# VectorE makes all low halves of the experts' weights and all one-hot tiles of the late plan

## The chip, the cores and the metric

The program runs on one core of a Trainium2 chip. The core has a matrix engine (TensorE, PE in the profile; its weight loads are PEld), VectorE (DVE), ScalarE (ACT), GpSimd (POOL), a queue engine that issues transfers (SyncE, SP) and 16 DMA engines. Each engine works through its own queue of instructions in order, and semaphores order the engines among each other. The metric is the device time of one execution in microseconds (us); lower is better.

## The reference

Three layers follow each other on 2304 tokens of width 512; everything is float32.

```python
scores = scale * q @ k.T, masked (local in 4 heads, strided in 4), softmax, @ v     # attention, 4 x 8 heads
h = x @ w_in; g = max(h, 0) + alpha * min(h, 0); x = g @ w_out                      # 512 -> 2048 -> 512
e_idx = argmax(x @ w_gate); gate_w = softmax value of that expert                   # 8 experts
out[tokens of e] = gate_w * sigmoid(x @ w_output_gate)[e] * (max(x @ w1[e], 0) @ w2[e])   # 512 -> 1024 -> 512
```

## The kernel before

A float32 product is made on TensorE as three products of split operands: each operand is written as a high half (rounded to the fast float format) and a low half (the difference), and high*high, low*high and high*low are summed. So each weight tile has to be split before it is used: ScalarE writes the high half by a copy, and another engine subtracts it from the raw tile.

The tokens go through the attention and the first MLP in six blocks of 384. As soon as five blocks are done, the routing is planned for them ("early" plan), and the last block follows while the first experts are at work ("late" plan). A plan ranks the tokens of each expert, gives each token a place in a list, and makes the lists by matmuls (function `lists`): for each of 18 (early: 15) tiles of 128 tokens a one-hot matrix of 128x128 (`onehot`, from the low part of the rank, `rank_lo`) is multiplied with a small matrix `aa`. The late plan is cut into five steps; the table `WHEN` says at which place of the loop over the experts each of them is written.

The experts are worked off in 16 places `t` in a fixed order: four early pairs of 128 tokens (kind P), then S0 Q0 S1 S2 P0 S3 Q1 P1 Q3 P2 Q2 S4. A P place has two lists of 128 tokens, an S place one, a Q place one of 32. For place `t` the loop writes the first product of place `t+1`, the second product of `t`, and the weight splits of `t+1` and `t+2`.

The weights of one expert are 4 MB: four raw tiles of 1 MB (`raws[0..3]`, one buffer each), loaded by SP in program order (`load_expert`, L884, skipped where the expert is the same as that of the place before). `split_expert(t, h)` splits one half of them into four tiles `wx`: ScalarE's copy (L891), then the subtraction (L893), which for `i == 3` is on GpSimd and else on VectorE. A raw tile can be loaded again when both subtractions of its two halves have read it, so raw tiles 1 and 3 wait for GpSimd. GpSimd's queue has the gathers of tokens (L900), the scatters of results (L1057) and 12 of the late plan's one-hot tiles (L794, `OHP`) as well; VectorE makes the other 6.

The names used below: `exh`, `exl` are the transposed tokens of a place (L911 transposes into the bank `sl_bank`, L924 writes the high half, L926 the low half), L955 to L959 and L970 to L972 are the first product (the middle one or the last one of three reads `exl` or the weights' low half), L994, L995, L1016 and L1017 split the hidden layer (`hh`, `hl`), L1015 transposes it into the banks X and T, L1047 is the second product, L806 the list matmuls.

Of the kernel before, what the change touches and what calls it, by code (L numbers as in the profile page):

```python
# [7 lines left out]
F32 = mybir.dt.float32  # L8
# [4 lines left out]
ALU = mybir.AluOpType  # L13
# [13 lines left out]
NTT = NT // P  # L27
BLK = 384
NBLK = NT // BLK
TPB = BLK // P  # L30
# [23 lines left out]
XA = 3  # L54

WHEN = ((0, 7), (1, 1), (1, 1), (1, 4), (1, 6))
OHP = 12

NRV = range(FIRST)
FS = {2: 2}  # L60
# [24 lines left out]
def attention_prelu_mlp_routed_experts_kernel(  # L85
# [11 lines left out]
    nc = tc.nc  # L97
# [28 lines left out]
    with tc.manual_schedule():  # L126
# [4 lines left out]
        def bank(tag, bufs=1):  # L131
            return ps.tile([P, 512], F32, tag=tag, name=tag, bufs=bufs)
# [3 lines left out]
        def half(tag):  # L136
            return sl_bank[:, 0:256] if tag == "S" else sl_bank[:, 256:512]
# [475 lines left out]
        def rank(blk):  # L613
            j0 = blk * TPB
            sl = slice(j0, j0 + TPB)

            def small(shape, name, dt=F32):
                return xpool.tile(shape, dt, tag=name, name=name, bufs=1)

            tmp = small([P, TPB, E], "r_tmp")  # L620
            pr_ = half("L") if blk < NBLK - 1 else bank("acc0")
            pr3 = pr_[:, : TPB * E]
            mm(pr3, u16, oh[:, sl, :].rearrange("p j e -> p (j e)"), start=True, stop=False)
            mm(pr3, one16, acc_oh[:, sl, :].rearrange("p j e -> p (j e)"), start=False, stop=True)
            rk = small([P, TPB], "r_rk")
            nc.vector.tensor_tensor(
                out=tmp, in0=pr3.rearrange("p (j e) -> p j e", e=E), in1=oh[:, sl, :], op=ALU.mult
            )
            nc.vector.tensor_reduce(out=rk, in_=tmp, axis=X, op=ALU.add)
            rh = rank_hi[:, sl]  # L630
            nc.vector.tensor_scalar(
                out=rh, in0=rk, scalar1=1.0 / P, scalar2=-63.5 / P, op0=ALU.mult, op1=ALU.add
            )
            nc.vector.tensor_scalar(out=rh, in0=rh, scalar1=BIG, scalar2=BIG, op0=ALU.add, op1=ALU.subtract)
            nc.vector.scalar_tensor_tensor(
                out=rank_lo[:, sl], in0=rh, scalar=-float(P), in1=rk, op0=ALU.mult, op1=ALU.add
            )

        plan_t = {}

        def plan_parts(early):
# [6 lines left out]
            nt = NTT - TPB if early else NTT  # L648
# [4 lines left out]
            def small(shape, dt=F32):  # L653
                n = 1
                for d in shape[1:]:
                    n *= d
                w = n if dt == F32 else (n + 1) // 2
                t = room[: shape[0], room_at[0] : room_at[0] + w]
                room_at[0] += w
                if dt != F32:  # L660
                    t = t.bitcast(dt)[:, :n]
                if len(shape) == 3:
                    t = t.rearrange("p (a b) -> p a b", b=shape[2])
                return t
# [46 lines left out]
            else:  # L711
# [8 lines left out]
                    out=two, in0=two, scalar1=2 * BIG, scalar2=2 * BIG, op0=ALU.add, op1=ALU.subtract  # L720
# [29 lines left out]
            if early:  # L750
                aa = small([P, nt, 2 * ns], BF16)
            else:
                room2 = stage()
                aa = room2[:, : nt * ns].bitcast(BF16).rearrange("p (a b) -> p a b", b=2 * ns)
# [4 lines left out]
                out=aa[:, :, ns:], in0=a, scalar1=cst[:, C_P1 : C_P1 + 1], scalar2=None, op0=ALU.mult  # L759
# [6 lines left out]
            def experts(c0, c1, cum):  # L766
                n = c1 - c0
                t = le[:, c0 - k0 : c1 - k0]
                tt(
                    t,  # L770
                    cum[0:1].unsqueeze(1).to_broadcast([1, n, E]),
                    isl[0:1, c0:c1].unsqueeze(2).to_broadcast([1, n, E]),
                    ALU.is_le,
                )
                r = ef[:, c0 - k0 : c1 - k0]
                nc.vector.tensor_reduce(out=r, in_=t, axis=X, op=ALU.add)
                nc.vector.tensor_scalar_min(e_i32[:, c0:c1], r, float(E - 1))
# [3 lines left out]
            else:  # L781
                experts(C_P, C_S, cum)
                experts(C_S, C_Q, cum1)
                experts(C_Q, NSLOT, cumq)
            yield
            tag, w = ("xg", DM + 1) if early else ("gh", BLK)
            k = 2 * w // P
            onehot = []
            for j in range(nt):
                if j % k == 0:  # L790
                    pool = epool if early else xpool
                    t = pool.tile([P, w], F32, tag=tag, name="onehot", bufs=XG if early else 3).bitcast(BF16)
                onehot.append(t[:, (j % k) * P : (j % k + 1) * P])
                (nc.vector if early or j >= OHP else nc.gpsimd).tensor_scalar(  # L794
                    out=onehot[j], in0=i128, scalar1=rank_lo[:, j : j + 1], scalar2=None, op0=ALU.is_equal
                )
            plan_t[early] = aa, small, onehot

        def lists(early):
            k0, k1 = (0, EARLY) if early else (EARLY, NSLOT)  # L800
# [85 lines left out]
        def split_expert(t, h, some=range(4)):  # L886
            for i in some:
                q = 4 * h + i
                raw = raws[q // 2][:, (q % 2) * 1024 : (q % 2) * 1024 + 1024]
                w = wx[t, q] = w_tile(NA, F32R, "wx")  # L890
                nc.scalar.activation(out=w[:, :1024], in_=raw, func=AF.Copy)  # L891
                eng = nc.gpsimd if i == 3 else nc.vector
                eng.tensor_tensor(out=w[:, 1024:], in0=raw, in1=w[:, :1024].bitcast(F32), op=ALU.subtract)  # L893

        xg_t, wt_t, xx_t, hp_t, hr_t, hh_t, po_t = {}, {}, {}, {}, {}, {}, {}

# [237 lines left out]
        for s in range(NPRO):  # L1134
# [5 lines left out]
            if s == 4:  # L1140
# [3 lines left out]
                    out=wg_hl[:, :, 2 * E :], in0=wg_sb, in1=wg_hl[:, :, : 2 * E].bitcast(F32), op=ALU.subtract  # L1144
# [149 lines left out]
        for t in range(NPL):  # L1294
            more = t + 1 < NPL
            wide_now = kinds[t] == "P"
            wide_next = more and kinds[t + 1] == "P"
            few_now = kinds[t] == "Q"
            few_next = more and kinds[t + 1] == "Q"
            if t < 2:  # L1300
                gathers(XA, EARLY // 2)
            else:
                gathers(XA)
            if wide_next:
                first_product(t + 1, range(2))
            if few_next:
                first_product(t + 1)
                if t + 2 < NPL:
                    load_expert(t + 2, 0)
            late_turn = few_now and more and not wide_next  # L1310
            if late_turn:
                first_product(t + 1)
                relu(t + 1, 0)
            nb = NB.get(kinds[t] + kinds[t + 1] + kinds[t + 2], 2) if t + 2 < NPL else 2
            split(t + 2, 0, range(nb))
            at(t, 1)
            early_x = wide_next and t + 2 < NPL and kinds[t + 2] == "Q"
            if early_x:
                turn_x(t + 2, 0)
            if more and not few_next and not late_turn:  # L1320
                first_product(t + 1, range(2, 4))
            at(t, 2)
            if late_turn:
                relu(t + 1, 1)
            if t + 2 < NPL and not early_x:
                turn_x(t + 2, 0)
            if late_turn:
                turn_h(t + 1)
            elif more and not wide_next:
                relu(t + 1)  # L1330
            elif more and not wide_now:
                relu(t + 1, 2)
                relu(t + 1, 3)
            split(t + 2, 0, range(nb, 4))
            at(t, 3)
            if not few_now:
                second_product(t, 0, 4)
            if few_next:
                turn_h(t + 1)
            at(t, 4)  # L1340
            if wide_now and wide_next:
                relu(t + 1, 2)
                relu(t + 1, 3)
            if t == 0:
                rank(NBLK - 1)
            if t + 2 < NPL and kinds[t + 2] == "P":
                turn_x(t + 2, 1)
            at(t, 5)
            if not few_now:
                second_product(t, 4, 8)  # L1350
            at(t, 6)
            if t == 3:
                others = value(idx_any)
            if not few_now:
                split(t + 1, 1)
                give(t)
            at(t, 7)
            if few_next:
                second_product(t + 1, 0, 8)
                if t + 2 < NPL:  # L1360
                    load_expert(t + 2, 1)
                if t > 2:
                    gathers(XA)
                split(t + 2, 1)
                give(t + 1)
            elif more and not wide_next and not late_turn:
                turn_h(t + 1)
# [132 lines left out]
```

## Time and profile before

| what | us |
|---|---|
| median of 3 runs | 815.4 (814.32 to 817.51) |
| the profiled execution | 815.9 |
| its span, first to last instruction | 814.0 |
| PE busy | 782.4 (96%) |
| DVE busy | 456.3 (56%) |
| ACT busy | 428.1 (53%) |
| POOL busy | 167.0 (21%) |

The rows below come from one profiled execution. Times of rows are counted from the start of the span. PE is busy nearly all the time, so the stretches where it is not are what there is to look for; a row of waits tells which engine ended them, and a timeline row what that engine did before.

### The profile page before, as it was taken

The numbers are of one execution on the slowest core, as the hardware profiler recorded it, in microseconds if no ns is written. First come the engines' busy times: TensorE is split into PE (matmuls) and PEld (weight loads), VectorE is DVE, ScalarE is ACT, GpSimd is POOL, SyncE is SP. The second block draws the span as 40 slices with busy tenths as digits, with TensorE's granted clock in tenths as the row PEclk, the third lists the DMA queues.
The fourth block names the chain that finished last, engine by engine and source line by source line (L and its number), as shares of the span: only waits on it lengthen the run. The fifth ranks groups of instructions, "written<-read, shape, count | busy, mean of one in ns | idle before, by whom it ended". The sixth has DMA issues, their size and how long they took to land. (4 is left out here: it accounts for less than half of the span.)

```text
span 814.0 us, 13678 instructions
## 1 busy us (share of the span) xinstructions
PE 782.4 (96%) x5046; PEld 657.5 (81%) x5050; DVE 456.3 (56%) x1005; ACT 428.1 (53%) x1057; POOL 167.0 (21%) x127
## 2 busy tenths in 40 slices
PE   8888999999999999999999999999989998999995
PEld 4566778888888888888888888899879876878884
DVE  5989994345434544545334335566695447854422
ACT  6867875554445454645333343364444566665542
POOL 0001111010101010111000000133365454536422
PEclk9899999999999999999999999999999999999998
DMA  9719212012100120101000001635033677777520
GB/s 342 312 50 365 79 39 79 1 38 81 65 0 19 68 84 32 47 1 40 1 0 19 22 1 40 246 117 177 19 106 141 212 253 273 268 276 267 182 83 32
DMA packets 22621, 91.05 MB, mean 112 GB/s; under 512 B 3082, under 2 KB 7312, under 8 KB 15376
## 3 DMA queue, kind: packets, MB, share of 16 engines
q1 hardware_dynamic: 18816, 78.52, 27.4%
q0 software_dynamic: 3728, 11.55, 4.0%
q8 instruction: 42, 0.69, 0.4%
q14 instruction: 35, 0.29, 0.1%
HBM read 105.78 MB, written 9.97 MB: 142 GB/s over the span
## 5 line engine op out<-in xcount | busy, mean ns | idle before, releaser
L444 PE MATMUL h<-xh,w 128*128 128x384 f32 x384 | 129.8, 338 | 1.1 <-DVE gl L465 0.8
L445 PE MATMUL h<-xl,w 128*128 128x384 f32 x384 | 129.2, 337 | 0.7 <-DVE xl L373 0.7
L446 PE MATMUL h<-xh,w 128*128 128x384 f32 x384 | 129.2, 336 | 0.0
L893 DVE TENSOR_TENSOR wx<-raw,wx 128x1024 fp32r<-128x1024 f32 x72 | 97.0, 1391 | 50.0 <-ACT wx L891 49.7
L478 PE MATMUL acc<-w,gh 128*128 128x512 f32 x288 | 124.8, 433 | 0.0
L455 DVE SCALAR_TENSOR_TENSOR h<-h,nalpha,a 128x384 f32<-128x384 f32 x96 | 59.9, 624 | 114.8 <-ACT h L454 114.7
L480 PE MATMUL acc<-w,gl 128*128 128x512 f32 x288 | 114.2, 397 | 0.0
L479 PE MATMUL acc<-w,gh 128*128 128x512 f32 x288 | 113.9, 396 | 0.0
L298 POOL TENSOR_TENSOR p<-p,sm 96x512 f32<-96x512 f32 (+2 forms) x38 | 35.6, 937 | 345.0 <-DVE sm L297 239.5
L453 ACT ACTIVATE a<-h 128x384 f32<-128x384 f32 x96 | 47.1, 491 | 103.1 <-PE h L446 103.1
L891 ACT ACTIVATE wx<-raw 128x1024 fp32r<-128x1024 f32 x96 | 94.6, 1056 | 10.7 <-DMA raw<-in_wexp_dram 10.7
L1047 PE MATMUL acc<-wx,hh 128*128 128x512 f32 x304 | 96.7, 399 | 0.0
L893 POOL TENSOR_TENSOR wx<-raw,wx 128x1024 fp32r<-128x1024 f32 x24 | 63.5, 2647 | 93.0 <-ACT wx L891 92.9
L444 PEld LDWEIGHTS h<-xh,w 128*128 128x128 f32 x384 | 72.4, 189 | 6.5 <-DVE gl L465 1.8
L445 PEld LDWEIGHTS h<-xl,w 128*128 128x128 f32 x384 | 72.3, 188 | 4.8 <-DVE xl L373 1.0
L446 PEld LDWEIGHTS h<-xh,w 128*128 128x128 f32 x384 | 72.2, 188 | 0.0
L465 DVE TENSOR_TENSOR gl<-h,gh 128x384 fp32r<-128x384 f32 x96 | 53.2, 554 | 32.0 <-PE acc L480 17.1
L1047 PEld LDWEIGHTS acc<-wx,hh 128*128 128x128 f32 x304 | 56.4, 191 | 11.1
L480 PEld LDWEIGHTS acc<-w,gl 128*128 128x128 f32 x288 | 54.5, 189 | 13.1
L464 ACT ACTIVATE gh<-h 128x384 fp32r<-128x384 f32 x96 | 46.8, 487 | 33.4 <-DVE h L455 33.1
L478 PEld LDWEIGHTS acc<-w,gh 128*128 128x128 f32 x288 | 54.2, 188 | 10.6 <-issue 0.3
L1047 PE MATMUL acc<-wx,hl 128*128 128x512 f32 x152 | 60.1, 395 | 0.0
(259 smaller groups left out, 1473.7 us busy)
## 6 DMA issues: line engine op xcount, KB each, us to landing
raw<-in_wexp_dram SPq DMA_DIRECT2D x64, 1024.0 KB
raw<-in_wp_dram SPq DMA_DIRECT2D x16, 1024.0 KB
qk<-in_qkv_dram SPq DMA_DIRECT2D x10, 576.0 KB
rows<-stage SPq DMA_DIRECT2D x15, 256.5 KB
v<-in_qkv_dram SPq DMA_DIRECT2D x8, 320.0 KB
qk<-in_qkv_dram SPq DMA_DIRECT2D x4, 384.0 KB
v<-in_qkv_dram SPq DMA_DIRECT2D x6, 256.0 KB
qk<-in_qkv_dram SPq DMA_DIRECT2D x4, 224.0 KB
```

The lines of the kernel that those rows point to most:

```text
L444: mm(ph[:, :BLK], w_in(c, 0, k), xh[:, k, :], start=(k == 0), stop=False)
L445: mm(ph[:, :BLK], w_in(c, 0, k), xl[:, k, :], start=False, stop=False)
L446: mm(ph[:, :BLK], w_in(c, 1, k), xh[:, k, :], start=False, stop=(k == KD - 1))
L453: nc.scalar.activation(out=a, in_=v, func=AF.Relu)
L455: nc.vector.scalar_tensor_tensor(out=v, in0=v, scalar=nalpha[:, c : c + 1], in1=a, op0=ALU.mult, op1=ALU.add)
L465: nc.vector.tensor_tensor(out=gl, in0=v, in1=gh.bitcast(F32), op=ALU.subtract)
L478: mm(o, gh[:, t], w_out(c, 0), start=(c == 0), stop=False)
L479: mm(o, gh[:, t], w_out(c, 1), start=False, stop=False)
L480: mm(o, gl[:, t], w_out(c, 0), start=False, stop=(c == NC1 - 1))
L891: nc.scalar.activation(out=w[:, :1024], in_=raw, func=AF.Copy)
L893: eng.tensor_tensor(out=w[:, 1024:], in0=raw, in1=w[:, :1024].bitcast(F32), op=ALU.subtract)
L1047: mm(po[i], h[:, h0 : h0 + P], wk[:, w0 : w0 + 512], start=st, stop=sp)
```

## The change

GpSimd makes no low half and no one-hot tile any more. Every `i == 3` subtraction goes to VectorE, directly behind that of `i == 2`. The one-hot tiles are made by a function of its own, `onehots`, which can be called twice: the first call, in place `t == 0` just ahead of the ranking of the last block, makes the fifteen tiles of the first five blocks (their ranks are known by then); the second, where they all stood, makes the three of the last block.

```diff
-OHP = 12
...
+            onehots(early, nt)
+            plan_t[early] = aa, small, onehot_t[early]
+
+        onehot_t = {True: [], False: []}
+        onehot_in = {}
+
+        def onehots(early, nt):
+
             tag, w = ("xg", DM + 1) if early else ("gh", BLK)
             k = 2 * w // P
-            onehot = []
-            for j in range(nt):
+            onehot = onehot_t[early]
+            for j in range(len(onehot), nt):
                 if j % k == 0:
                     pool = epool if early else xpool
                     t = pool.tile([P, w], F32, tag=tag, name="onehot", bufs=XG if early else 3).bitcast(BF16)
+                    onehot_in[early] = t
+                t = onehot_in[early]
                 onehot.append(t[:, (j % k) * P : (j % k + 1) * P])
-                (nc.vector if early or j >= OHP else nc.gpsimd).tensor_scalar(
+                nc.vector.tensor_scalar(
                     out=onehot[j], in0=i128, scalar1=rank_lo[:, j : j + 1], scalar2=None, op0=ALU.is_equal
                 )
-            plan_t[early] = aa, small, onehot
...
-                eng = nc.gpsimd if i == 3 else nc.vector
-                eng.tensor_tensor(out=w[:, 1024:], in0=raw, in1=w[:, :1024].bitcast(F32), op=ALU.subtract)
+                nc.vector.tensor_tensor(out=w[:, 1024:], in0=raw, in1=w[:, :1024].bitcast(F32), op=ALU.subtract)
...
             if t == 0:
+                onehots(False, NTT - TPB)
                 rank(NBLK - 1)
```

On VectorE, in place `t == 0` between the low halves of the hidden layer (`hl`) and the late plan's first step (`stage` is the plan's workspace), this stood in a row before:

```order
L995 SCALAR_TENSOR_TENSOR hl<-T,hh 128x512
L626 TENSOR_TENSOR r_tmp<-acc_5968,oh 128x24
L629 TENSOR_REDUCE r_rk<-r_tmp 128x3
L631 TENSOR_SCALAR rank_hi<-r_rk 128x3
L634 TENSOR_SCALAR rank_hi<-rank_hi 128x3
L635 SCALAR_TENSOR_TENSOR rank_lo<-rank_hi,r_rk 128x3
L925 COPY wt<-xg 128x1
L926 TENSOR_TENSOR exl<-sl_bank,exh 128x4x128
L893 TENSOR_TENSOR wx<-raw,wx 128x1024 x3
L668 TENSOR_SCALAR stage<-acc_6034 128x8
```

And this stands there now (line numbers are those of the changed kernel):

```order
L1002 SCALAR_TENSOR_TENSOR hl<-T,hh 128x512
L803 TENSOR_SCALAR onehot<-cst_65,rank_lo 128x128 x15
L625 TENSOR_TENSOR r_tmp<-acc_5986,oh 128x24
L628 TENSOR_REDUCE r_rk<-r_tmp 128x3
L630 TENSOR_SCALAR rank_hi<-r_rk 128x3
L633 TENSOR_SCALAR rank_hi<-rank_hi 128x3
L634 SCALAR_TENSOR_TENSOR rank_lo<-rank_hi,r_rk 128x3
L932 COPY wt<-xg 128x1
L933 TENSOR_TENSOR exl<-sl_bank,exh 128x4x128
L900 TENSOR_TENSOR wx<-raw,wx 128x1024 x4
L667 TENSOR_SCALAR stage<-acc_6052 128x8
```

Fifteen one-hot tiles now stand ahead of the ranking, of `exl` of place 2 and of the split of the weights, and that split has four subtractions where it had three.

At the end of the late plan's third step, still on VectorE, this stood before:

```order
L777 TENSOR_SCALAR e_i_4284<-stage 1x8
L794 TENSOR_SCALAR onehot<-cst_65,rank_lo 128x128 x6
L925 COPY wt<-xg 128x1
L926 TENSOR_TENSOR exl<-sl_bank,exh 128x4x128
L893 TENSOR_TENSOR wx<-raw,wx 128x1024
```

and now:

```order
L776 TENSOR_SCALAR e_i_4284<-stage 1x8
L803 TENSOR_SCALAR onehot<-cst_65,rank_lo 128x128 x3
L932 COPY wt<-xg 128x1
L933 TENSOR_TENSOR exl<-sl_bank,exh 128x4x128
L900 TENSOR_TENSOR wx<-raw,wx 128x1024 x2
```

Three one-hot tiles are left here, and the split that follows has one subtraction more.

GpSimd's queue around the same places was, from the first gathers of place 1 on:

```order
L900 DMA xg<-rows,idx_in 128x513
L893 TENSOR_TENSOR wx<-raw,wx 128x1024 x2
L605 DMA rows<-stage 128x513 x3
L900 DMA xg<-rows,idx_in 128x513 x3
L893 TENSOR_TENSOR wx<-raw,wx 128x1024 x2
L1057 DMA out_dram<-stage,idx_out 2304x512 x2
L900 DMA xg<-rows,idx_in 128x513
L794 TENSOR_SCALAR onehot<-cst_65,rank_lo 128x128 x12
L893 TENSOR_TENSOR wx<-raw,wx 128x1024 x2
L1057 DMA out_dram<-stage,idx_out 2304x512 x2
```

and is now:

```order
L907 DMA xg<-rows,idx_in 128x513 x4
L604 DMA rows<-stage 128x513 x3
L907 DMA xg<-rows,idx_in 128x513 x3
L1064 DMA out_dram<-stage,idx_out 2304x512 x2
L907 DMA xg<-rows,idx_in 128x513
L1064 DMA out_dram<-stage,idx_out 2304x512 x2
```

Only transfers are left in it; their order among themselves is the same. The queues of PE, ACT and SP hold the same instructions in the same order as before.

## Rows read from the trace of the kernel before

**Rows 1.** Busy time by stretch: length, engines' busy time (instructions), PE clock, DMA share, GB/s.

```profile
600.00:606.50 6.50, 3.19 (x26) 2.02 (x26) 6.29 (x19) 1.08 (x2) 4.91 (x6) 1.00 0.47 158
606.50:609.90 3.40, 3.40 (x11) 2.83 (x11) 3.06 (x7) 2.52 (x4) 0.00 (x0) 0.50 0.42 94
665.00:684.00 19.00, 15.44 (x72) 11.82 (x73) 12.56 (x12) 11.82 (x17) 10.91 (x6) 1.00 0.91 319
684.00:700.00 16.00, 14.33 (x102) 13.07 (x101) 14.77 (x14) 12.73 (x17) 9.82 (x5) 1.00 0.72 245
700.00:798.00 98.00, 98.00 (x795) 83.01 (x794) 46.40 (x53) 53.74 (x75) 42.23 (x26) 1.00 0.58 199
```

**Rows 2.** Waits of PE from 560 us on: sum, times, longest (us).

```profile
PE acc L957 <- DVE wx L893: 1.6, 1, 1.6
PE X L970 <- DVE hl L1017: 1.5, 1, 1.5
PE T L1015 <- ACT hr L988: 1.2, 2, 1.0
PE acc L959 <- DVE exl L926: 1.0, 1, 1.0
```

**Rows 3.** The low halves, line 893: durations in ns (min/median/max), first and last start.

```profile
L893 DVE TENSOR_TENSOR wx<-raw,wx x72: 1207/1219/3422, 530.5 to 795.4; 128x1024 fp32r<-128x1024 f32 x72
...
L893 POOL TENSOR_TENSOR wx<-raw,wx x24: 2327/2537/3200, 533.4 to 796.4; 128x1024 fp32r<-128x1024 f32 x24
```

**Rows 4.** Timeline of PE, list matmuls: start, us, instruction [idle before <-who ended it].

```profile
601.18 0.53 PE L806 MATMUL acc<-stage,onehot 128*128 128x76 bf16 x10
...
605.02 0.86 PE L806 MATMUL acc<-stage,onehot 128*128 128x76 bf16 x5 [2.12 <-DVE onehot L794]
606.33 0.80 PE L911 MATMUL sl_bank<-cst,xg 128*128 128x128 f32 x3 [0.45 <-DVE exl L926]
```

**Rows 5.** Timeline of VectorE at the early plan and at the late one.

```profile
512.35 2.51 DVE L794 TENSOR_SCALAR onehot<-cst,rank_lo 128x128 bf16<-128x128 bf16 x15
...
581.22 5.67 DVE L893 TENSOR_TENSOR wx<-raw,wx 128x1024 fp32r<-128x1024 f32 x3
...
599.53 0.50 DVE L758 TENSOR_SCALAR stage<-stage,cst 128x684 bf16<-128x684 bf16 x1
...
601.90 3.71 DVE L794 TENSOR_SCALAR onehot<-cst,rank_lo 128x128 bf16<-128x128 bf16 x6
```

**Rows 6.** Timeline of GpSimd: one-hot tiles and low halves.

```profile
592.64 9.96 POOL L794 TENSOR_SCALAR onehot<-cst,rank_lo 128x128 bf16<-128x128 bf16 x12
602.58 2.33 POOL L893 TENSOR_TENSOR wx<-raw,wx 128x1024 fp32r<-128x1024 f32 x1
...
662.17 2.39 POOL L893 TENSOR_TENSOR wx<-raw,wx 128x1024 fp32r<-128x1024 f32 x1
...
675.98 2.38 POOL L893 TENSOR_TENSOR wx<-raw,wx 128x1024 fp32r<-128x1024 f32 x1 [1.68 <-ACT wx L891]
```

**Rows 7.** Timeline of PE: where the low halves of places 2 and 8's tokens are first read.

```profile
584.12 0.28 PE L971 MATMUL h<-exl,wx 128*128 128x256 f32 x1
...
689.34 0.38 PE L971 MATMUL h<-exl,wx 128*128 128x256 f32 x1
```

**Rows 8.** Timeline of SP's queue around 664 us: three loads.

```profile
664.59 1.42 SPq L884 DMA_DIRECT2D raw<-in_wexp_dram  x3
```

**Rows 9.** Timeline of ACT at the same place.

```profile
665.51 3.91 ACT L891 ACTIVATE wx<-raw 128x1024 fp32r<-128x1024 f32 x4 [1.66 <-DMA raw<-in_wexp_dram]
```

**Rows 10.** Timeline of VectorE, 660 to 697 us.

```profile
660.08 1.21 DVE L893 TENSOR_TENSOR wx<-raw,wx 128x1024 fp32r<-128x1024 f32 x1
...
676.34 3.10 DVE L893 TENSOR_TENSOR wx<-raw,wx 128x1024 fp32r<-128x1024 f32 x1
...
688.60 0.68 DVE L926 TENSOR_TENSOR exl<-sl_bank,exh 128x512 fp32r<-128x512 f32 x1
689.39 7.06 DVE L893 TENSOR_TENSOR wx<-raw,wx 128x1024 fp32r<-128x1024 f32 x3
```

## The prediction

> **What bounds the kernel now.** I read the busy times by stretch first. From 700 to 798 us PE is busy for all 98 of 98 us, so nothing can be gained there but by starting it earlier. Three stretches before it are not full: 600 to 606.5 (3.19 of 6.50 busy, 3.31 lost), 665 to 684 (15.44 of 19.00, 3.56 lost) and 684 to 700 (14.33 of 16.00, 1.67 lost). Right behind the first one the granted clock is 0.50, the lower of the two levels (1.2 GHz), for 3.4 us, which costs half of that, 1.7 us [rows 1]. So what the change can move is 3.3 + 3.6 + 1.7 of waiting and 1.7 of clock, 10.2 us; the rest of PE's work it doesn't touch.
>
> Next the waits say who ends those gaps. In the first it is VectorE's one-hot tiles (2.12 us at once), then 0.45 for `exl` [rows 4]. In the others it is VectorE again (`wx` 1.6, `hl` 1.5, `exl` 1.0) and once ScalarE (`hr`) [rows 2].
>
> The timelines then say why VectorE was late, and it is not for want of time: it stood still beside GpSimd. A low half takes it 1.22 us in the median, but up to 3.42 [rows 3]. Three halves that would take 3.7 us took 7.06 from 689.39 on and 5.67 from 581.22 on; one took 3.10 from 676.34 on [rows 10, 5], while GpSimd was at its own from 675.98 to 678.36 [rows 6]. The six one-hot tiles of the late plan took 3.71 us, and GpSimd's low half ran through their middle (602.58 to 604.91); fifteen of the early plan, with GpSimd at rest, took 2.51, or 0.167 each [rows 5, 6].
>
> **The change part by part.** *The low halves.* GpSimd loses 24 of 2.54 us, VectorE gains 24 of 1.22, 29 us, and gets back what the collisions cost. That sum says little; what counts is each place. In a split the fourth half now follows the third on VectorE, so it is done about 1.2 us behind it, where GpSimd's needed 2.5 from ScalarE's copy on, and more where a gather was ahead of it in its queue. What stands behind a split on VectorE (`exl`, `hl`) comes 1.2 us later wherever there was no collision, and earlier where there was one. From 700 us on I cost this at nothing: VectorE is busy for 46 of 98 us there, the added halves bring some 15, and PE never waited [rows 1]; if that cover were gone, each `exl` would cost up to 1.2.
>
> *The first fifteen one-hot tiles.* They stand ahead of the ranking, of `exl` of place 2 and of a split. At 0.167 each they take 2.51 us. `exl` was done when the split began, at about 581.3, and comes at 583.8; PE first reads it at 584.12 [rows 5, 7]. So it is hidden, with 0.3 us to spare. This is the tightest of the costs that I take as nothing: a shade more per tile and PE waits. The nearest rows bound the tile at 0.167 and at 3.71/6 = 0.62; nothing of GpSimd's runs there any more, so I take 0.167.
>
> *The late plan.* The split behind them begins at 583.7 instead of 581.22 and takes 4 x 1.22 = 4.9 instead of 5.67, so it ends at 588.6 instead of 586.9. All steps of the plan, which follow on VectorE, move back by 1.7. `aa`, ready at 600.03, is ready at 601.75; PE gets to the list matmuls at 601.18 [rows 4, 5] and waits 0.6 for it. Then it does the first fifteen, whose tiles are long there. The last three tiles start at 603.6 (601.90 + 1.7) and end at 604.1; the copy and `exl` behind them (0.75) end at 604.85, and the transpose that waits for it, at 606.33 before, starts at 605.0. That is 1.3 to 1.7 gained (the second, if consecutive halves overlap a little), and I take 1.5: most of the wait for the tiles goes, but a wait for the plan itself is next behind it.
>
> *The clock.* It fell behind a single wait of 2.12 followed by 0.45. It did not fall after the waits of 1.6 and 1.5 us [rows 1, 2]. The longest new wait is some 1.5 (from the fifteenth list matmul to the sixteenth), so I take it that the clock stays at 2.4 GHz: 1.7 gained. Bounds are 0 and 1.7.
>
> *665 to 684.* Here loads set the pace (DMA share 0.91, 319 GB/s). SP sends in order; its load at 664.59 waited for GpSimd's half of 662.17 to 664.56, and with it the two issues behind it, and ScalarE waited 1.66 for those before its copies at 665.51 [rows 1, 6, 8, 9]. VectorE's third half of that split ended at 661.29 [rows 10], so a fourth ends at 662.5: the load leaves 2.1 us sooner, and the copies start about 1.1 sooner (their data also waits for PE). The waits for `hr` (1.0 at the longest), `exl` (1.0) and `wx` (1.6, behind the 3.10) all go, 3.56. But the stream of loads moves by 2.1 only, and the split of place 8 waits for it. Behind that split stands `exl` of place 8, which was done at 689.28 and read at 689.34 [rows 7, 10]. Sooner by 2.1 for the loads, by the collision's end a little more, later by 1.2 for the fourth half, with ScalarE's copies back to back ahead of it: it comes some 2.3 sooner, and PE, which would be there 3.56 sooner, waits 1.2 for it. I take 2.3; bounds are 3.56 (it is not late) and -1.2 (the loads come no sooner, and only the fourth half tells).
>
> *684 to 700.* Four halves from `exl` on at 1.22 are 4.9 us instead of the 7.06 and what GpSimd did beside them. `hl` comes 2.2 + 2.3 sooner in time, PE 2.3, so the 1.5 us wait goes, and the 0.2 beside it: 1.6. "Perfetto Trace Analysis" in the Trainium skill (section Optimizing Scalar/DVE Operations) would speak against this: with VectorE saturated, it says, some work may well be handed to ScalarE or even GpSimd. VectorE shows 14.77 us busy of 16.00 in this stretch [rows 1]. By that rule the two halves of GpSimd's that run there (2.4 us) fill it to 17.2, PE waits 1.2 more, and the sum would be smaller by 2.8. By the rows, 3.4 of the 14.77 is the standing still in the 7.06, and without it 13.8 are needed. The page adds in the same place that the two engines share a read port, so that handing work over might not help; the stretched halves agree.
>
> *The sum* is 1.5 + 1.7 + 2.3 + 1.6 = 7.1 us. From 700 on PE only starts sooner, and all of it reaches the end. Against the profiled execution's own 815.9 (span 814.0, 1.9 around it) that is 808.8; that execution lies 0.5 above the median of the runs, 815.4, from which it would be 808.3. I predict 808.5.
>
> **The rivals.** *All waits go.* If the load stream moves as far as PE, and plan and `exl` are in time, 10.2 us are saved: 815.9 - 10.2 = 805.7. For it: each wait named has a collision behind it. Against it: plan and loads have paces of their own, as worked out.
>
> *The loads keep the pace.* If the stream from 665 to 684 is bound by its bandwidth (0.91 busy), the earlier issue at 664.59 only makes it wait elsewhere. Then `exl` of place 8 comes 1.2 later than before; the 1.5 us wait behind it goes; together 0.3 gained instead of 3.9. With the clock falling as before (the wait is only spread out) 1.5 + 0.3 = 1.8 are left: 814.1, or 813.6 off the median. For it speaks the 0.91; against it the ScalarE wait of 1.66 for an issue that was held up by GpSimd and not by bytes.
>
> *The fifteen tiles block the way: slower.* If a tile costs 0.62 in the first place as in the late one, the row takes 9.3 us, `exl` of place 2 ends at 590.6 and PE waits 6.5 from 584.12, with a second fall of the clock (1.7). The split then ends at 595.4, 8.5 later, and the three last tiles at 601.90 + 8.5 + 1.9 = 612.3; with `exl` behind them the transpose comes at 613.2, 6.9 later than before, the 6.5 in it. Less 3.9 from the stretches behind: 815.9 + 6.9 + 1.7 - 3.9 = 820.6. It begins to cost from 0.19 a tile (2.8 us to spare over fifteen) and makes the whole slower from about 0.4. For it: the six that took 3.71, and that the added row stands ahead of everything of VectorE's. Against it: in those six one was held by GpSimd, and the fifteen at 512 us were not.
>
> That the change doesn't do what it says needs no price: the queues show the fifteen and the three, and GpSimd with transfers alone.
>
> **How the numbers follow.** The forecast gets 0.58, all waits gone 0.13, the loads 0.22, the blocking tiles 0.07. About 0.5% (4.1 us) is what a measurement of this kernel can tell from no change, so faster means under 811.3. The forecast's own range is 806.8 (`exl` of place 8 in time, the plan at its better end) to 810.5 (the clock falls as before); both lie under that line, as does 805.7. The loads' case lies within it, the blocking tiles' case beyond 819.5 just so. That gives faster 0.71, same 0.22, slower 0.07. The range runs from 805.0, a little under the case without waits, to 813.8, the loads' case off the median.
>
> **What would show it.** In the profile of the changed kernel the 96 low halves of VectorE have a longest of about 1.25 us. The fifteen tiles take about 2.5 us in one row at some 580 us, and PE doesn't wait at its next `exl`. PE's gap at the list matmuls is 2 to 2.5 us in two or three pieces, ended by `aa`, by the last tiles and by `exl`; the clock stays up behind it. Between 665 and 690 one wait of about 1 us for `exl` of place 8 is left, and the waits for `wx` and `hl` are gone. From 700 on PE is full. I am wrong if VectorE's halves stay long beside GpSimd's transfers, if PE waits behind the fifteen tiles, or if new waits for `exl` show up from 700 on.

## The result and the profile after

| | before | after |
|---|---|---|
| median of the 7 runs taken together, us | 815.22 (813.45 to 817.84) | 808.43 (808.12 to 812.18) |
| profiled execution, us | 815.9 | 808.35 |
| its span, us | 814.0 | 806.6 |

The ratio is 0.9913, with a 95% interval from 0.9892 to 0.9934: 0.87% faster, and clear of the noise. The forecast was 808.5.

The page's busy times of the kernel after; PE had 782.4 us before, and GpSimd now has little left:

```profile
PE 779.9 (97%) x5050; PEld 655.1 (81%) x5050; DVE 469.7 (58%) x1041; ACT 427.8 (53%) x1057; POOL 90.9 (11%) x91
```

The low halves first (line 893 is L900 now, one-hot tiles are L803, `exl` is L933, the list matmuls are L814, the transposes of the hidden layer L1022). Durations in ns, as in [rows 3]:

```profile
L900 DVE TENSOR_TENSOR wx<-raw,wx x96: 1203/1218/1300, 530.7 to 789.8; 128x1024 fp32r<-128x1024 f32 x96
```

The median is where it was, and the longest has come down from 3422 to 1300. VectorE has 24 halves and 12 tiles more and is busy for only 13.4 us more (469.7 against 456.3).

VectorE's timeline at the places of [rows 5] and [rows 10]:

```profile
578.25 2.53 DVE L803 TENSOR_SCALAR onehot<-cst,rank_lo 128x128 bf16<-128x128 bf16 x15
...
581.66 0.68 DVE L933 TENSOR_TENSOR exl<-sl_bank,exh 128x512 fp32r<-128x512 f32 x1
582.26 4.62 DVE L900 TENSOR_TENSOR wx<-raw,wx 128x1024 fp32r<-128x1024 f32 x4
...
599.12 0.40 DVE L757 TENSOR_SCALAR stage<-stage,cst 128x684 bf16<-128x684 bf16 x1
...
601.35 0.56 DVE L803 TENSOR_SCALAR onehot<-cst,rank_lo 128x128 bf16<-128x128 bf16 x3
...
683.49 4.62 DVE L900 TENSOR_TENSOR wx<-raw,wx 128x1024 fp32r<-128x1024 f32 x4
688.03 0.68 DVE L1024 TENSOR_TENSOR hl<-X,hh 128x512 fp32r<-128x512 f32 x1
```

Four halves now take 4.62 us where three took 5.67 and 7.06. The fifteen tiles take 2.53, or 0.169 each, and `exl` behind them ends at 582.34, 0.4 us before PE reads it (its L978 starts at 582.73, without a wait). `aa` (the 0.40 at 599.12) is ready at 599.5, before PE comes to the lists.

PE's waits from 550 us on, which answer to [rows 2] (sum, times, longest):

```profile
PE acc L814 <- DVE onehot L803: 1.2, 1, 1.2
PE h L978 <- DVE exl L933: 1.0, 1, 1.0
PE T L1022 <- ACT wx L899: 0.7, 1, 0.7
PE sl_bank L918 <- DVE exl L933: 0.4, 1, 0.4
PE T L1022 <- ACT hr L995: 0.2, 1, 0.2
```

And the same stretches as in [rows 1]; the later ones start sooner by what PE had gained up to them:

```profile
600.00:606.50 6.50, 4.89 (x29) 3.75 (x27) 6.29 (x21) 4.07 (x6) 0.00 (x0) 0.74 0.56 185
...
661.50:680.50 19.00, 18.29 (x88) 14.48 (x88) 14.26 (x16) 14.41 (x21) 3.27 (x3) 1.00 0.82 298
680.50:693.30 12.80, 11.82 (x96) 11.37 (x95) 12.31 (x15) 9.39 (x13) 4.26 (x3) 1.00 0.91 345
693.30:791.00 97.70, 97.70 (x785) 82.25 (x785) 51.73 (x62) 53.70 (x75) 19.21 (x16) 1.00 0.53 193
```

PE stands idle for 1.61 us at the lists (6.50 - 4.89; 3.31 before), for 0.71 in the next stretch (3.56) and for 0.98 in the one behind it (1.67), and is full from there on. That is 1.7 + 2.85 + 0.69 = 5.24 us.

At the lists the gain is larger than the idle time tells. PE's timeline there:

```profile
599.79 0.70 PE L814 MATMUL acc<-stage,onehot 128*128 128x76 bf16 x15
601.65 0.53 PE L814 MATMUL acc<-stage,onehot 128*128 128x76 bf16 x3 [1.16 <-DVE onehot L803]
602.63 0.67 PE L918 MATMUL sl_bank<-cst,xg 128*128 128x128 f32 x4 [0.45 <-DVE exl L933]
```

From the first list matmul to the transpose behind them it is 2.84 us now (599.79 to 602.63) and was 5.15 (601.18 to 606.33 [rows 4]): 2.3 less, where the idle time gives 1.7. The matmuls come in two groups instead of four and keep PE busy for 0.6 less.

In these two profiles the granted clock gives the rest. In the middle of the program it fell to 0.50, the level of 1.2 GHz, twice before, for 3.4 us each, and once after. Two windows of the kernel after, and one of the kernel before:

```profile
555.00:563.00 8.00, 8.00 (x71) 8.00 (x70) 6.68 (x26) 2.63 (x7) 0.24 (x1) 1.00 0.68 264
...
603.15:606.56 3.41, 3.41 (x11) 2.64 (x10) 3.38 (x8) 3.23 (x4) 0.00 (x0) 0.50 0.92 329
```

```profile
558.69:562.10 3.41, 3.41 (x18) 3.41 (x18) 2.40 (x16) 0.43 (x2) 0.00 (x0) 0.50 0.87 312
```

So the fall behind the lists is still there (at 606.5 before, 603.15 now), and one at 558.7 is gone, behind 24 small matmuls of the last block's expert choice, where the change moves nothing of PE's. At half speed for 3.4 us, one fall costs 1.7 us. With 2.3 + 2.85 + 0.69 = 5.8 that makes 7.5; the span is shorter by 7.4.

That is one execution of each kernel, and the runs do not bear out the share of the clock. The mean granted clock of a whole run is on average 0.9890 over the 7 runs of the kernel after, and 0.9891 and 0.9883 over the 23 and the 14 runs of the kernel before that stand beside the experiments (falls anywhere in the run count in it). A thousandth of it is worth some 0.8 us (an estimate, 0.001 of 815 us), so the clock gives the kernel after less than 1 us over its runs, and nothing against the 23. Of the 6.8 us between the two medians 5.8 are placed without it, and the rest stays open.

### The profile page after: what moved, and what is told of

It reads as the page before. It is cut to its first block, busy times and chain, and to the rows that moved or that the text cites. A ratio compares the mean times of both kernels' runs of the same rounds, so it can differ in the third digit from the quotient of the medians.

```text
span 806.6 us, 13674 instructions
## 1 busy us (share of the span) xinstructions
PE 779.9 (97%) x5050; PEld 655.1 (81%) x5050; DVE 469.7 (58%) x1041; ACT 427.8 (53%) x1057; POOL 90.9 (11%) x91
## 4 chain that ended last, share of the span: by engine, by line
PE 77%; DVE 12%; issue 4%; ACT 3%; DMA 3%; SPq 0%; another core or an unknown queue 0%; POOL 0%; ACTq 0%; POOLq 0%; DVEq 0%
PE acc L1054 10%; PE acc L477 8%; PE h L444 7%; PE h L443 7%; PE h L445 7%; PE acc L479 7%; PE acc L478 7%; PE T L328 2%; PE sl_bank L234 2%; DMA raw<-in_wp_dram 2%; DVE stage L407 2%; PE T L313 2%; PE h L977 1%; DVE w L424 1%; PE h L978 1%
## 5 line engine op out<-in xcount | busy, mean ns | idle before, releaser
L900 DVE TENSOR_TENSOR wx<-raw,wx 128x1024 fp32r<-128x1024 f32 x96 | 112.1, 1220 | 41.5 <-ACT wx L899 38.2
L477 PEld LDWEIGHTS acc<-w,gh 128*128 128x128 f32 x288 | 54.3, 189 | 10.6 <-issue 0.3
L478 PEld LDWEIGHTS acc<-w,gh 128*128 128x128 f32 x288 | 54.8, 190 | 5.5
```

What stands on the lines that cost most here:

```text
L477: mm(o, gh[:, t], w_out(c, 0), start=(c == 0), stop=False)
L478: mm(o, gh[:, t], w_out(c, 1), start=False, stop=False)
L900: nc.vector.tensor_tensor(out=w[:, 1024:], in0=raw, in1=w[:, :1024].bitcast(F32), op=ALU.subtract)
```

## The experiments

The theory: VectorE's subtractions, which read two tiles of SBUF, stood still while GpSimd's subtractions read there, so the gain is the end of these collisions. Rivals: the gain is in the one-hot tiles (GpSimd was late with 12 of them, or they now come early); or in GpSimd itself, on whose late halves loads and PE waited. The median of the kernel before that stands beside halves_only, tiles_only, idle_reads and tiles_late is 816.33 us, that beside the other four 815.88; the ratios are against these.

**halves_only**: the kernel before, with the low halves alone moved.

```diff
-                eng = nc.gpsimd if i == 3 else nc.vector
-                eng.tensor_tensor(out=w[:, 1024:], in0=raw, in1=w[:, :1024].bitcast(F32), op=ALU.subtract)
+                nc.vector.tensor_tensor(out=w[:, 1024:], in0=raw, in1=w[:, :1024].bitcast(F32), op=ALU.subtract)
```

> All low halves on VectorE, the one-hot tiles as before (12 on GpSimd, 6 on VectorE at the late place). My theory: the gain comes from the end of the standing still of the two engines beside each other, so the halves alone bring nearly all of it. Between 665 and 700 us 3.9 as in the changed kernel, and at the list matmuls as well, since no half of GpSimd's runs through VectorE's six tiles any more and the plan begins 1 us sooner: 807 to 810 us, longest half about 1.3 us outside GpSimd's tiles. Rival, the tiles carry the gain: 812 or more, with the 3.3 us of waiting at the list matmuls still there.

Measured 806.89 us, 0.9890 [0.9869, 0.9911]: all of the gain, a shade under the range that was expected. GpSimd still makes 12 of the 18 tiles, and PE does not wait for a tile at all. Its timeline at the lists:

```profile
601.15 1.53 PE L806 MATMUL acc<-stage,onehot 128*128 128x76 bf16 x18
...
603.13 0.66 PE L910 MATMUL sl_bank<-cst,xg 128*128 128x128 f32 x4 [0.45 <-DVE exl L925]
```

The same 18 matmuls had a wait of 2.12 us in them before [rows 4] and have one of 1.16 in the kernel after. So it was the halves that made the tiles late, and the edits to the tiles are not needed.

**tiles_only**: the kernel after, with GpSimd's share of the halves put back.

```diff
+                eng = nc.gpsimd if i == 3 else nc.vector
-                nc.vector.tensor_tensor(out=w[:, 1024:], in0=raw, in1=w[:, :1024].bitcast(F32), op=ALU.subtract)
+                eng.tensor_tensor(out=w[:, 1024:], in0=raw, in1=w[:, :1024].bitcast(F32), op=ALU.subtract)
```

> The one-hot tiles as in the changed kernel, the fourth halves back on GpSimd. My theory: the collisions stay, the plan comes some 2 us later behind the fifteen tiles and a held half, the 5 us of waits between 665 and 700 us stay: 813.5 to 816. Rival, the tiles carry the gain: 808 to 810.

Measured 816.5 us, 1.0008 [0.9993, 1.0023]: nothing gained, and 0.5 above the expected range. The halves are as long as before, and at the lists it is now the plan that is late. The reason is not the one expected: the split behind the fifteen tiles ends at 586.9, as in the kernels before and after. It is a later step of the plan that stands still, beside GpSimd's half of 596.38 to 599.76; it takes 3.05 us, 0.87 in the kernel after. So work of VectorE's other than the low halves is held as well. Durations, that step, and some of PE's waits:

```profile
L901 DVE TENSOR_TENSOR wx<-raw,wx x72: 1201/1219/3423, 530.0 to 795.4; 128x1024 fp32r<-128x1024 f32 x72
```

```profile
597.43 3.05 DVE L676 TENSOR_TENSOR stage<-cst,stage 128x684 bf16<-128x684 bf16 x1
```

```profile
PE acc L814 <- DVE stage L757: 2.5, 1, 2.5
...
PE X L978 <- DVE hl L1025: 1.5, 1, 1.5
PE acc L814 <- DVE onehot L803: 1.4, 1, 1.4
```

**idle_reads** parts the theory from the second rival. It is the kernel after, and behind every fourth half GpSimd subtracts that tile's high half from itself, in two pieces, into a tile that nobody reads. Nothing waits for GpSimd's result.

```diff
+                if i == 3:
+                    for f in (0, 512):
+                        hi = w[:, f : f + 512].bitcast(F32)
+                        nc.gpsimd.tensor_tensor(out=spare[0], in0=hi, in1=hi, op=ALU.subtract)
```

> The changed kernel, and beside it GpSimd subtracts, where its fourth half was, ScalarE's high half from itself into a spare tile that nothing reads (two subtractions of 512 columns each). No result and no load waits for it. Theory of the collision: VectorE's halves are held again (longest 2.5 us or more), the waits of PE for wx, hl or exl between 665 and 700 us come back, and the time is 811 to 818 us. Rival, the gain came from GpSimd's half being late for its readers and for the loads: nothing waits for these, so 808 to 809.

Measured 816.0 us, 1.0002 [0.9989, 1.0015]: the whole gain is lost again. The longest half is 2.07 us and not the 2.5 or more that was expected; GpSimd's pieces are half as long, so VectorE stands still for shorter at a time. Durations of both engines' instructions, and then the halves as a group (busy time, mean ns):

```profile
L901 DVE TENSOR_TENSOR wx<-raw,wx x96: 1203/1224/2065, 530.6 to 796.9; 128x1024 fp32r<-128x1024 f32 x96
...
L905 POOL TENSOR_TENSOR spare<-wx x48: 1037/1446/2015, 533.4 to 798.0; 128x512 f32<-128x512 f32 x48
```

```profile
L901 DVE TENSOR_TENSOR wx<-raw,wx 128x1024 fp32r<-128x1024 f32 x96 | 133.2, 1441 | 36.3 <-ACT wx L900 33.9 <-issue 2.2
```

The mean of a half is 1441 ns, 1220 in the kernel after. PE's waits come back in the three stretches in which the kernel before had them. These are the longest, all for VectorE:

```profile
PE acc L814 <- DVE stage L757: 2.7, 1, 2.7
PE h L983 <- DVE exl L938: 1.8, 1, 1.8
PE X L982 <- DVE hl L1029: 1.2, 1, 1.2
PE acc L971 <- DVE exl L938: 1.1, 1, 1.1
PE acc L814 <- DVE onehot L803: 1.0, 1, 1.0
```

**idle_writes**: the same places, but GpSimd writes there (four fills of 128x512) and reads but one column.

```diff
+                if i == 3:
+                    nc.gpsimd.tensor_copy(spare[0][:, 0:1], w[:, 0:1].bitcast(F32))
+                    for _ in range(4):
+                        nc.gpsimd.memset(spare[0], 0.0)
```

> The changed kernel, and beside it GpSimd at the places of its fourth halves copies one column and then writes zeros four times into a spare tile of 512 columns (nothing reads it). It works as long as before but hardly reads. Theory that it is GpSimd's reading that holds VectorE's halves with their two inputs from the same memory: halves keep their 1.22 us, 808 to 809.5. Rival, any work of GpSimd holds them: 811 to 818, as with the idle subtractions.

Measured 808.94 us, 0.9919 [0.9890, 0.9948]: the gain stays. Durations:

```profile
L901 DVE TENSOR_TENSOR wx<-raw,wx x96: 1203/1218/1235, 530.4 to 789.8; 128x1024 fp32r<-128x1024 f32 x96
...
L905 POOL MEMSET spare<- x96: 525/527/602, 534.0 to 791.8; 128x512 f32 x96
```

GpSimd is kept busy for some 2.1 us (4 x 0.527) at each of the 24 places, and no half is longer than 1.235 us. Its transfers stand behind this work as they do in idle_reads, so it is not their delay that cost the gain there. What is left of the differences is that GpSimd subtracts and reads in one kernel and fills in the other, and of these the reading is the likely one. That is what "SBUF — State Buffer" in the Trainium skill states (section Who interferes with whom): a VectorE instruction with two inputs in SBUF contends with a GpSimd instruction that reads SBUF, not with one that only writes it. The two runs agree, with 2065 against 1235 ns for the longest half.

**tiles_late**: the kernel after without the call at the first place, so that all 18 tiles are made on VectorE at the late one.

```diff
-                onehots(False, NTT - TPB)
```

> The changed kernel with all eighteen tiles in a row at the late place. My theory: VectorE does the same work ahead of the transpose that waits for exl, only in another order, so that transpose comes at the same time: 808 to 809.5 us. Rival, the first place is what pays: the fifteen tiles are 2.5 us more at the late place, 810 to 811.

Measured 808.08 us, 0.9911 [0.9893, 0.9929], the same as the kernel after. PE's waits have none at the list matmuls:

```profile
PE h L978 <- DVE exl L933: 1.2, 1, 1.2
PE sl_bank L918 <- DVE exl L933: 0.4, 1, 0.4
```

The first place brings nothing. With all 18 tiles late, each is ready about as PE comes to it: the 18 matmuls are spread over 2.45 us, without one long wait.

**halves_6_to_8** asked whether what is gained at 665 to 700 can be had there alone: the kernel before, with the halves of places 6 to 8 moved (six, not the five that the expectation speaks of; 18 stay on GpSimd).

```diff
-                eng = nc.gpsimd if i == 3 else nc.vector
+                eng = nc.gpsimd if i == 3 and not 6 <= t <= 8 else nc.vector
```

> The kernel before with only the fourth halves of places 6, 7 and 8 (five of the 24 splits, the run of S places from 665 to 700 us) on VectorE; tiles as before. My theory: the waits of 5.2 us there shrink to about 1.5 as in the changed kernel and nothing else moves, so 3.5 to 4 us are gained: 811.5 to 813. Rival, the gain in that stretch needs the sooner start at the list matmuls or the halves of the places around it: 814 to 816.

Measured 813.8 us, 0.9961 [0.9945, 0.9977]: less than expected. PE's three longest waits:

```profile
PE acc L806 <- DVE onehot L794: 2.1, 1, 2.1
PE h L970 <- ACT exh L924: 1.3, 1, 1.3
PE h L971 <- DVE exl L926: 1.2, 1, 1.2
```

The wait at the lists stays, as it should, but 1.3 + 1.2 us are still waited for the tokens of place 8, against 1.0 in the kernel after, and the clock falls behind them (at 688.3). ScalarE's copies ahead of these tokens waited 1.42 and 0.53 us for loads (from 679.7 us on), and not at all in the kernel after; why the loads are late there stays open. The granted clock is lower too, 0.9871 over its runs against 0.9883, worth some 1 us by the estimate above. So this run is half a miss.

**plan_behind** tried to take away the waits that are left at the lists: the kernel after, with the three late tiles made right behind the ranking, and the plan's step `experts` behind the first product's turn.

```diff
-WHEN = ((0, 7), (1, 1), (1, 1), (1, 4), (1, 6))
+WHEN = ((0, 7), (1, 1), (1, 8), (1, 8), (1, 4), (1, 6))
...
+            at(t, 8)
             split(t + 2, 0, range(nb, 4))
...
+            if t == 0:
+                onehots(False, NTT)
```

> The changed kernel with the late plan in another order: the last three tiles right behind the ranking of the last block, and the step that finds the experts' numbers (2 us on VectorE) behind exl of place 3 instead of ahead of it. My theory: of the waits of 1.16 and 0.45 at the list matmuls and the transpose behind them 1.2 to 1.6 go: 806.5 to 807.5; the clock then has less reason to fall there, up to 1.7 more. Rival, the plan itself is late for PE: 808 and over.

Measured 805.77 us, 0.9870 [0.9848, 0.9892], 0.7 under the expected range. Between the lists' matmuls and behind them PE no longer waits:

```profile
602.30 0.79 PE L815 MATMUL acc<-stage,onehot 128*128 128x76 bf16 x18
```

Its runs spread from 804.19 (mean granted clock 0.996) to 811.7 (0.987), and its profiled execution is one of the longer ones (span 809.9; two waits of 1.2 for the tokens of place 8, as in halves_6_to_8, and a fall of the clock behind them at 686.6). Its runs have a mean granted clock of 0.992 on average, the kernel after 0.989; by the estimate above that is 2.4 of the 2.7 us by which its median is lower. So the waits at the lists are gone, but that the new order makes the kernel faster than the kernel after is not shown.

**orders_mended** starts from halves_only, the simpler kernel: the plan's steps are written in an order in which `exl` does not wait for `experts`, and where two S places are followed by a P place, the split of the P place is cut in two and its second part written behind the turn of its tokens.

```diff
-WHEN = ((0, 7), (1, 1), (1, 1), (1, 4), (1, 6))
+WHEN = ((0, 7), (1, 1), (1, 1), (1, 8), (1, 4), (1, 6))
...
-            split(t + 2, 0, range(nb, 4))
+            at(t, 8)
+            ssp = "".join(kinds[t : t + 3]) == "SSP"
+            split(t + 2, 0, range(nb, 2 if ssp else 4))
...
+            if ssp:
+                split(t + 2, 0, range(2, 4))
```

> The low halves alone on VectorE (tiles as before), with two orders mended: the step that finds the experts' numbers stands behind exl of place 3, and the last two halves of place 8's first split stand behind the exl of place 8 that PE waited 0.97 us for. My theory: the waits of 0.45 and 0.97 go, 1.2 to 1.5 less than with the halves alone, so 805 to 806. Rival, ScalarE or the loads are late next and the waits only move: 806.5 to 807.5.

Measured 805.58 us, 0.9870 [0.9849, 0.9892], span 803.7: the lowest median of all, with GpSimd still making 12 tiles. Three waits of PE are left, two of them in one row:

```profile
PE T L1015 <- ACT hr L988: 1.0, 2, 0.7
PE X L970 <- DVE hl L1017: 0.5, 1, 0.5
```

Its interval overlaps that of halves_only, so the step from 806.89 to 805.58 is likely rather than shown (it is not the clock, which is 0.990 on average here and 0.9915 there); that it beats the kernel after is clearer (0.9870 against 0.9913, the intervals meeting at their ends).

## Why the prediction was right

*The mechanism* was the one named: VectorE stood still beside GpSimd. halves_only and tiles_only put the whole gain on the halves, idle_reads gives it back by work that nobody needs, idle_writes does not. The rule on a saturated VectorE in "Perfetto Trace Analysis" of the Trainium skill, weighed in the prediction, would have made the sum smaller by 2.8. The trace did not follow it: in the stretch from 680.5 to 693.3 VectorE is fuller than before, busy for 12.31 of 12.80 us, and PE waits 0.98 instead of 1.67.

*The late plan*: 1.5 foretold, as the time by which the transpose behind the lists comes sooner. Counted like that from the first list matmul on, 2.3 were measured, and 1.7 of them as idle time. One piece had been left out: ahead of the 2.12 PE also waited twice for GpSimd's own tiles, which the profile of the kernel before has as

```profile
PE acc L806 <- POOL onehot L794: 0.7, 2, 0.4
```

and these waits went as well. The working was partly another, too: the plan was not late (`aa` at 599.5 and not 601.75), so the 0.6 for it did not come. The split ended at 586.9, not at 588.6; of these 1.7 us 1.4 are owed to the fall of the clock that is missing at 558.7, since all that stands ahead of the split comes sooner by that. But PE came to the lists sooner by as much (599.79, not 601.18). What made the plan early for PE is that the four halves took 4.62 and not 4.9, and that its steps that had run beside GpSimd's tiles are shorter now (`aa` 0.40 us; 0.50 in [rows 5]). idle_writes, which has the fall, shows the same: `aa` is ready at 600.82 and PE comes at 601.08. The last three tiles came at 601.35, not at 603.6, and cost 1.16. And the term is due to the halves: without the tile edits the wait is shorter still.

*The fifteen tiles*: 2.51 foretold, 2.53 measured, hidden as foretold. The slower rival asked for 0.4 a tile.

*665 to 700*: 2.3 + 1.6 = 3.9 foretold, 2.85 + 0.69 = 3.5 measured. `exl` of place 8 is waited for, 1.2 foretold and 0.98 measured (it falls into the second stretch). The waits for VectorE's `wx` and for `hl` are gone. What came in their place is 0.7 for ScalarE's copy. SP's queue and ScalarE's timeline at that place, which answer to [rows 8] and [rows 9]:

```profile
658.76 1.82 SPq L892 DMA_DIRECT2D raw<-in_wexp_dram  x2
...
663.37 1.18 SPq L892 DMA_DIRECT2D raw<-in_wexp_dram  x2
```

```profile
660.65 2.01 ACT L899 ACTIVATE wx<-raw 128x1024 fp32r<-128x1024 f32 x2 [0.45 <-DMA raw<-in_wexp_dram]
...
663.52 2.01 ACT L899 ACTIVATE wx<-raw 128x1024 fp32r<-128x1024 f32 x2 [0.86 <-DMA raw<-in_wexp_dram]
```

The loads that stood at 664.59 go at 658.76. PE is some 3.8 us ahead by then, so about 2 us of that are sooner for PE, as foretold (2.1). ScalarE waits 0.45 + 0.86 for loads instead of 1.66. So the rival in which the loads keep the pace is out for this kernel: it gave 0.3 for these stretches. But the next pair goes only at 663.37, and for some 2.3 us of that the profile names no engine of the core that SP waited for. In tiles_late PE's wait of 0.7 is absent. Why SP stood there stays open. Nor are the loads out of the way in every kernel: in halves_6_to_8 and plan_behind they are waited for at place 8.

*The clock* is the step that failed: "I take it that the clock stays at 2.4 GHz: 1.7 gained". It fell at 603.15, behind waits of only 1.16 and 0.45 us. In the profile the total holds because the fall at 558.7 was missing instead, which nobody foretold; over the runs the clock gave less than 1 us, and the lists gave 0.8 more than foretold. So the mechanism was right, and that the sum of 7.1 came out so near is in part luck. I compared the ten profiles (the kernels before and after and the eight above). From 500 us on each has a first fall of the clock, either near 559 or between 602 and 603.2, and the change does not decide at which: halves_only, idle_writes and orders_mended have it near 559 as the kernel before has, tiles_late near 602 as the kernel after has, with no wait of over 0.45 us at the lists; idle_writes waits there as the kernel after does (1.2 and 0.4) and keeps the clock up. The four kernels with a wait of 2 us or more at the lists (before, tiles_only, idle_reads, halves_6_to_8) have 3.4 us more of the low clock there: a second fall at 606.4, or one of 6.8 us from 602.4. No other has that there. This goes with a long wait costing one fall, of the size that the term had; only the other fall was overlooked. It is read from one profile of each kernel and no run takes it apart, so it is not shown, and what sends the first fall to the one place or the other stays open.

*From 700 us on* nothing was lost, as foretold. The added halves there are nine (GpSimd's from 707.03 to 796.39 us before), some 11 us of VectorE's and not 15; nothing hung on it.

*All waits go* did not come: 3.5 us of waits are left from 550 on.

## What to carry to other kernels

Where a second engine takes a share of one kind of work, compare the longest with the median duration of that operation and look at what the other engine did in the long ones: busy time that is really standing still makes an engine seem short of time (14.77 us busy of 16.00 here) when giving it more work can be the cure. Test it with a kernel in which the helper does the same reads for nobody. And try each edit of a change alone: here one edit, the engine of the fourth halves, held the whole gain, and the others none.

## What was not expected of the hardware

GpSimd is held too, in work that is not arithmetic. From 500 us on, its issue of an indirect transfer takes 0.94 to 1.15 us in every profile when no low half of VectorE's runs beside it. Beside the low halves it takes anything from 0.95 to 2.31 us in the kernel after, and once 5.31 in plan_behind (585.21 us). So the halves are not always in its way, and no run here takes apart when they are. GpSimd's timeline of the kernel after, the first of these beside the four halves of 683.49:

```profile
686.69 2.31 POOL L1064 DMA_INDIRECT out_dram<-stage,idx_out  x1 [17.36 <-ACT hh L1023]
689.30 0.99 POOL L907 DMA_INDIRECT xg<-rows,idx_in  x1 [0.30 <-DVE hl L1024]
```

Where GpSimd's own halves met VectorE's, the price was paid on both sides: VectorE's half went from 1.22 to as much as 3.42 us, GpSimd's from 2.33 to 3.20 [rows 3].
